# A cycle's first score bank read by ScalarE and VectorE in turn, in a fused attention and mixer kernel

## The chip, the cores and the metric

The kernel runs on one core of one Trainium2 chip. The metric is device microseconds of one execution; lower is better. Engines are named as in the profile: PE is TensorE's matmuls and PEld its weight loads, ACT is ScalarE, DVE is VectorE, POOL is GpSimd, SP is SyncE, which issues most DMAs.

## The reference, cut to what matters

The output is a gated sum of an attention branch (16 heads of 28 over 2048 tokens, one shared key and value head) and a token and channel mixer. The change lies in the attention alone:

```python
q = (x @ wq).reshape(B, S, H, Dh)...      # B, S, D, H = 1, 2048, 448, 16; Dh = 28
k = x @ wk
v = x @ wv
scores = jnp.einsum("bhqd,bkd->bhqk", q, k) * (Dh ** -0.5)
p = _softmax(scores, axis=-1)
o = jnp.einsum("bhqk,bkd->bhqd", p, v)
a = (o in token order).reshape(B, S, H * Dh) @ wo
return g * a + (1 - g) * b                # g = sigmoid(x . gate_w), b the mixer branch
```

## The kernel before

The first 390 us compute the projections and the mixer; they are the same in both kernels. The rest is attention, in 16 units `u` (four blocks of 512 queries by four groups of four heads). A unit has 16 key tiles of 128 keys. A cycle `c` handles two of them, so a unit is eight cycles `i` = 0 to 7, and there are 128 cycles (`NC`).

All engines run in the order in which the code is written; no scheduler reorders it. The score products of one key tile give four banks of 128 keys by 512 queries, one for each head, from three fp32r products each (L207: `qh,kh`, `ql,kh`, `qh,kl`). Eight banks of PSUM are in play: four single banks `s0` to `s3` (the profile names all of them `bank`) and two pairs (`pair`). Singles swap roles from cycle to cycle: this cycle's `s2, s3` are the next one's `s0, s1`.

A cycle does this:

1. PE: scores of the even tile into `s0`, `s1` and the first pair (twelve products); then scores of the odd tile into `s2`, `s3` and the second pair.
2. ACT: the exponentials of `s0`, `s1` (L260, into the tile `pa`), of `s2`, `s3` and the second pair (into `pb`), and last of `pa[:, both]` in place in SBUF, 1024 columns.
3. DVE copies the first pair raw into `pa[:, both]` (L1033), which is what ACT's last step then works on.
4. PE: the products with the values of the two key tiles of the cycle before (L969), for the left 256 queries into `s0[:, 0:256]`, then for the right 256 into `s1[:, 0:256]`. These overwrite scores that the exponentials have read. Then a "job" into `s0[:, 256:480]`: an eighth of a unit's product with `wo` (L919), or, in cycles 2 to 11, a quarter row of a mixer product left over (112 columns wide).
5. DVE adds the two value results to the running sum `o` (L892, or L888 for the first of a unit), then the job's result (L936, or L955).

At `i` = 2 (`MAX_AT`) of each unit PE also computes bounds of the next unit's maxima into the first pair, and DVE reduces them.

VectorE also has side work, each piece at one cycle of a unit, between the copy of step 3 and the first addition of step 5: the end of the maxima at `i` = 3 (L249, L250 and a transpose, then eight DMAs on SP's queue); the reciprocal of the softmax sums at `i` = 1 (L902) with two instructions of a range check (L877, L878); the product `norm` with the reciprocals at `i` = 4 (L914); at `i` = 5 the high part of the queries of the unit after next (L196), at `i` = 6 their low part (L199, 512 columns), and right after that the four DMAs that fetch the following queries `qr` on SP's queue (L192). The reciprocal's input `rt` is a DMA on the same queue (L897), issued at the end of `i` = 0; its result goes out (`rd`, L906) and comes back spread over partitions (`rb`, L908).

Of the kernel before, what the change touches and what calls it, by code (L numbers as in the profile page):

```python
# [9 lines left out]
F32 = mybir.dt.float32  # L10
# [7 lines left out]
P = 128  # L18
# [19 lines left out]
def f32(ap):  # L38
    return ap.bitcast(F32)
# [3 lines left out]
def gated_mix_kernel(  # L43
# [13 lines left out]
    nc = tc.nc  # L57
# [137 lines left out]
        qh_of[u], ql_of[u] = qh, ql  # L195
        nc.vector.tensor_copy(qh, qr_of[u])  # L196

    def q_low(u):
        nc.vector.tensor_sub(ql_of[u], qr_of.pop(u), f32(qh_of[u]))  # L199

    def scores(u, kt, ps):
        kh = kh_of[0]
# [40 lines left out]
                nc.vector.reduce_max(mr[:, j, t:t + 1], mk, axis=AX.X)  # L243
        mx_of[u] = mr

    def max_end(u):
        mr = mx_of.pop(u).rearrange("p j t -> p (j t)")
        mc = late.tile([P, 32], F32R, tag="mc", bufs=2, name=f"mc_{u}")
        nc.vector.tensor_scalar(mc[:, 0:16], mr, -1.0, None, op0=ALU.mult)  # L249
        nc.vector.scalar_tensor_tensor(mc[:, 16:32], mr, -1.0, f32(mc)[:, 0:16],  # L250
                                       op0=ALU.mult, op1=ALU.subtract)
        mrow = late.tile([P, 32], F32, tag="mrow", bufs=2, name=f"mrow_{u}")
        nc.vector.transpose(mrow, f32(mc))
        for k in range(2):
            rows = f32(qh_of[u])[DH + k:P:32, :].rearrange("j (t p q) -> p j t q", p=4, q=32)
            for p in range(4):
                nc.sync.dma_start(rows[p], mrow[32 * p + 16 * k:32 * p + 16 * k + 16, :])
# [587 lines left out]
    with tc.tile_pool(name="s3", bufs=1, reuse_waits="tile") as s3, \  # L845
# [14 lines left out]
        def q_fetch(u):  # L860
            if u < NU:
                q_load(u, qr)
# [12 lines left out]
        def check(inverse, c):  # L875
            g = good[:, c:c + inverse.shape[1]]
            nc.vector.scalar_tensor_tensor(g, inverse, LIMIT, g, op0=ALU.is_le, op1=ALU.min)  # L877
            nc.vector.scalar_tensor_tensor(g, inverse, 1 / LIMIT, g, op0=ALU.is_ge, op1=ALU.min)  # L878
# [18 lines left out]
            nc.sync.dma_start(rt, o[0:128:32, :].rearrange("j (a b) -> j a b", b=16))  # L897
            return u, o, rt

        def recip(u, o, rt, checked=True):  # L900
            rr = s3.tile([P, 16], F32, tag="rr", bufs=2, name=f"rr_{u}")
            nc.vector.reciprocal(rr, rt)  # L902
            if checked:
                check(rr.rearrange("p (a b) -> p a b", b=4), 0)
            rd = dram.tile([4, 512], F32, tag="rd", bufs=2, name=f"rd_{u}")
            nc.sync.dma_start(rd.rearrange("j (a b) -> (j a) b", b=16), rr)  # L906
            rb = s3.tile([P, 512], F32, tag="rb", bufs=2, name=f"rb_{u}")
            nc.sync.dma_start(rb, rd.unsqueeze(1).broadcast_to([4, 32, 512]))  # L908
            return u, o, rb

        def norm(u, o, rb):
            on_of[u] = s3.tile([P, 512], F32, tag="on", bufs=2, name=f"on_{u}")
            for cols in (slice(0, 256), slice(256, 512)) if u == NU - 2 else (slice(0, 512),):
                nc.vector.tensor_mul(on_of[u][:, cols], o[:, cols], rb[:, cols])  # L914

        def by_columns(ps, a, t, w, start=True, stop=True):
            for i in range(4):
# [58 lines left out]
        jobs += [(w4_products, w4_add, (n // 4,), quarters[n % 4]) for n in range(2 * sum(JOBS_0), 16)]  # L976
        assert len(jobs) == sum(JOBS_0) + 10
        left, right, both, front = slice(0, 1), slice(1, 2), slice(2, 4), slice(0, 2)
        sums, norms, later = [], [], []
        pv = None  # L980
        MAX_AT = 2

# [13 lines left out]
        def run_jobs(ps, n):  # L996
            job_adds(job_products(ps, n))

        NC = NU * NT // 2
        HINTS = {8 * NT // 2 + 4: [mybir.EngineType.SP],  # L1000
                 14 * NT // 2 - 2: [mybir.EngineType.DVE, mybir.EngineType.Activation]}
        for c in range(NC):
            u, i = divmod(c, NT // 2)
            k = 2 * c
            s0, s1, s2, s3_ = singles if c % 2 == 0 else singles[2:] + singles[:2]
            if c == 0:
                pb = score_tiles(u, 1, s2, s3_, s0, s1)
                for j, ps in enumerate((s2, s3_, s0, s1)):
                    exps(pb, slice(j, j + 1), ps.unsqueeze(1))
                pa = score_tiles(u, 2, *(q[:, h] for q in pairs for h in range(2)))  # L1010
                nc.vector.tensor_copy(pa[:, front], pairs[0])
                for ps, n in zip((s2, s3_), JOBS_0):
                    run_jobs(ps, n)
                exps(pa, both, pairs[1])
                exps(pa, front)
                pairs.reverse()
                continue
            if c > 1:
                pa = score_tiles(u, 2 * i, s0, s1, pairs[0][:, 0], pairs[0][:, 1])
                with tc.block() if c in HINTS else nullcontext():  # L1020
                    if c in HINTS:
                        tc.mark_branch_hint_location("redo", "LikelyTaken", HINTS[c])
                    exps(pa, left, s0.unsqueeze(1))
                exps(pa, right, s1.unsqueeze(1))
            if i == 2 and u == 0:
                q_begin(1)
            if i == 3 and u == 0:
                q_low(1)
                q_fetch(2)
            if u == NU - 1 and i == 3:  # L1030
                norm(*norms.pop())
            if 1 < c < NC - 1:
                nc.vector.tensor_copy(pa[:, both], pairs[0])  # L1033
            elif c > 1:
                exps(pa, both, pairs[0])
            if i == 3 and later:
                later.pop(0)()
            if i == 1 and sums:
                norms.append(recip(*sums.pop()))
            if i == 4 and norms:  # L1040
                norm(*norms.pop())
            if i == 5 and u + 2 < NU:
                q_begin(u + 2)
            if i == 5 and u == 0:
                nc.sync.dma_start(wof, wo.rearrange("(g p) n -> p g n", p=P))
            if i == 6 and u + 2 < NU:
                q_low(u + 2)
                q_fetch(u + 3)
            pb = score_tiles(u, 2 * i + 1, s2, s3_, pairs[1][:, 0], pairs[1][:, 1])
            exps(pb, left, s2.unsqueeze(1))  # L1050
            exps(pb, right, s3_.unsqueeze(1))
            exps(pb, both, pairs[1])
            if 1 < c < NC - 1:
                exps(pa, both)
            if u and i == (3 if u == NU - 1 else 4):
                jobs += [(wo_products, wo_add, (u - 1, t), cols) for t in range(4) for cols in halves]
            v = (c - 1) // (NT // 2)
            at_max = i == MAX_AT and u + 1 < NU
            q0, q1 = slice(0, 256), slice(256, 512)
            values((k - 2, k - 1), s0[:, q0], q0)  # L1060
            values_end(v, s0[:, q0], q0)
            if at_max:
                max_part(u + 1, range(4), pairs[0][:, 0])
                later.append(lambda u=u: max_end(u + 1))
            elif i == MAX_AT:
                run_jobs(pairs[0][:, 0], 1)
            values((k - 2, k - 1), s1[:, q0], q1)
            adds = job_products(s0[:, q1], 0 if c == 1 else 1)
            values_end(v, s1[:, q0], q1)
            if i == 0 and v < NU - 1:  # L1070
                sums.append(sums_begin(v))
            job_adds(adds)
# [75 lines left out]
        with tc.If(again > 0, label="redo"):  # L1148
            for b in range(NB):
                for g in range(NG):  # L1150
                    u = b * NG + g
                    q_fetch(u)
                    q_begin(u)
                    q_low(u)
                    max_full(u, bank)
                    max_end(u)
                    pv = banks.pop(0)
                    for kt in range(NT):
                        ps = [bank(f"s2_{u}_{kt}_{j}") for j in range(4)]
                        scores(u, kt, ps)  # L1160
                        p = s3.tile([P, 4, 512], F32, tag="p", bufs=PB, name=f"p2_{u}_{kt}")
                        for j in range(4):
                            exps(p, slice(j, j + 1), ps[j].unsqueeze(1))
                        for j in range(4):
                            nc.tensor.matmul(pv[32 * j:32 * j + 32, :], vext[:, kt, :], p[:, j],
                                             start=(kt == 0), stop=(kt == NT - 1), tile_position=(0, 32 * j))
                    values_end(u, pv)
                    banks.append(pv)
                    norm(*recip(*sums_begin(u), False))
# [59 lines left out]
```

## Time and profile before

| | before |
|---|---|
| median of 3 runs | 903.35 us (902.7 to 903.94) |
| the profiled execution's own time | 903.46 us |
| its span, first to last instruction | 901.7 us |
| PE busy in the span | 896.0 us (99%) |
| ACT busy | 629.8 us (70%) |
| DVE busy | 527.5 us (58%) |
| granted TensorE clock, mean | 0.999 |

The profile is of one execution. Its timeline rows give a start in microseconds, a duration, the engine, the line, the operation, the tiles and how many instructions are merged into the row; in square brackets stands how long the engine had been idle and what ended that. A busy PE need not be at its peak, since the ends of matmuls are modelled: a wait of TensorE is seen at the weight loads (PEld) and in the distance between the starts of its matmuls.

### The profile page before, as it was taken

What the parts mean: (1) busy time and instruction counts of PE and PEld (TensorE: products, weight loads), DVE (VectorE), ACT (ScalarE), POOL (GpSimd) and SP (SyncE); (2) the same over time, 40 slices, a digit from 0 to 9 for tenths busy, and PEclk for the clock granted to TensorE, in tenths of its full rate; (3) what the DMA queues carried; (4) which work ended last, traced back from release to release, by engine and by line L of the source; (5) the groups of instructions that cost most, each with busy time, mean ns of one, the idle gap of its engine ahead of it and who ended that gap; (6) DMA issues with size and microseconds to landing.
All of it is one profiled execution on the core that took longest, in us unless ns stands there. A gap on an engine that the chain in (4) does not pass through costs nothing.

```text
span 901.7 us, 24214 instructions
## 1 busy us (share of the span) xinstructions
PE 896.0 (99%) x10396; PEld 628.0 (70%) x10396; DVE 527.5 (58%) x983; ACT 629.8 (70%) x1002; POOL 70.5 (8%) x109
## 2 busy tenths in 40 slices
PE   9999999999999999999999999999999999999998
PEld 7898988888888888865555555555555555555554
DVE  5575555643342431156776776677667667777665
ACT  5453354322132231279999999999999999999995
POOL 1123300700000520020000000000000000000000
PEclk9999999999999999999999999999999999999999
DMA  9977755400300300001000001000011000010001
GB/s 309 332 173 207 201 180 129 108 1 1 88 2 1 88 0 1 1 22 55 25 15 25 13 25 46 24 25 16 25 34 41 20 15 25 15 56 14 15 15 44
DMA packets 50474, 54.77 MB, mean 61 GB/s; under 512 B 11804, under 2 KB 38028, under 8 KB 50252
## 3 DMA queue, kind: packets, MB, share of 16 engines
q1 hardware_dynamic: 47580, 47.74, 19.0%
q10 hardware_dynamic: 2784, 5.46, 1.6%
q8 instruction: 82, 1.34, 0.6%
q14 instruction: 28, 0.23, 0.1%
HBM read 36.35 MB, written 15.33 MB: 57 GB/s over the span
## 4 chain that ended last, share of the span: by engine, by line
PE 97%; ACT 1%; DMA 0%; DVE 0%; issue 0%
PE bank L969 26%; PE bank L207 19%; PE bank L919 5%; PE acc L769 5%; PE acc L767 5%; PE acc L768 5%; PE g L138 4%; PE g L139 4%; PE g L140 4%; PE pair L207 3%; PE hs L530 1%; PE hs L529 1%; PE g L141 1%; PE g L142 1%; ACT p L260 1%; PE hs L532 1%
## 5 line engine op out<-in xcount | busy, mean ns | idle before, releaser
L260 ACT ACTIVATE p<-bank 128x512 f32<-128x512 f32 x514 | 266.5, 608 | 4.5 <-POOL pick L942 1.5
L969 PE MATMUL bank<-p,vext 128*32 128x256 f32 x4064 | 247.6, 382 | 0.5
L969 PEld LDWEIGHTS bank<-p,vext 128*32 128x32 f32 x4064 | 117.6, 109 | 116.0 <-ACT p L260 52.8
L1033 DVE COPY p<-pair 128x1024 f32<-128x1024 f32 x125 | 153.0, 1224 | 57.2 <-PE pair L207 43.4
L757 ACT ACTIVATE gh<-g 128x512 fp32r<-128x512 f32 x55 | 32.9, 598 | 184.1 <-PE g L142 184.1
L892 DVE TENSOR_TENSOR o<-o,bank 128x256 f32<-128x256 f32 x222 | 93.5, 421 | 80.5 <-PE bank L969 70.3
L260 ACT ACTIVATE p<-p 128x1024 f32<-128x1024 f32 x126 | 138.3, 1097 | 0.0
L260 ACT ACTIVATE p<-pair 128x1024 f32<-128x1024 f32 x129 | 136.8, 1061 | 0.0
L759 DVE TENSOR_TENSOR gl<-gf,gh 128x512 fp32r<-128x512 f32 x55 | 40.5, 737 | 160.6 <-ACT gf L758 160.6
L207 PE MATMUL bank<-qh,kh 32*128 32x512 f32 x514 | 114.7, 444 | 0.0
L207 PE MATMUL pair<-qh,kh 32*128 32x512 f32 x510 | 114.0, 443 | 0.0
L207 PE MATMUL bank<-qh,kl 32*128 32x512 f32 x514 | 101.6, 389 | 0.0
L207 PE MATMUL bank<-ql,kh 32*128 32x512 f32 x514 | 101.3, 390 | 0.0
L207 PE MATMUL pair<-qh,kl 32*128 32x512 f32 x510 | 101.0, 389 | 0.0
L207 PE MATMUL pair<-ql,kh 32*128 32x512 f32 x510 | 100.5, 389 | 0.0
L207 PEld LDWEIGHTS bank<-qh,kh 32*128 32x128 f32 x514 | 47.4, 181 | 60.1 <-issue 38.1
L769 PE MATMUL acc<-w4h,gl 128*128 128x448 f32 x220 | 80.7, 367 | 0.0
L767 PE MATMUL acc<-w4h,gh 128*128 128x448 f32 x220 | 80.1, 364 | 0.0
L768 PE MATMUL acc<-w4l,gh 128*128 128x448 f32 x220 | 79.8, 363 | 0.0
L919 PE MATMUL bank<-wof,on 128*32 128x224 f32 (+1 forms) x976 | 68.9, 356 | 0.0
L138 PE MATMUL g<-ah,w3h 128*128 128x512 f32 x168 | 65.4, 389 | 0.0
L139 PE MATMUL g<-al,w3h 128*128 128x512 f32 x168 | 65.4, 389 | 0.0
(205 smaller groups left out, 1388.4 us busy)
## 6 DMA issues: line engine op xcount, KB each, us to landing
rb<-rd SPq DMA_DIRECT2D x15, 256.0 KB
x<-in_x_dram SPq DMA_DIRECT2D x4, 896.0 KB
hd<-raws SPq DMA_DIRECT2D x16, 224.0 KB
hraw<-hd SPq DMA_DIRECT2D x4, 896.0 KB
w34raw<-in_w_dram SPq DMA_DIRECT2D x7, 512.0 KB
qr<-qd SPq DMA_DIRECT2D x64, 56.0 KB
w34raw<-in_w_dram SPq DMA_DIRECT2D x7, 448.0 KB
out_dram<-ot SPq DMA_DIRECT2D x14, 224.0 KB
```

Source lines behind the costliest of these rows:

```text
L138: nc.tensor.matmul(ps, wh[:, c, :], ah[:, c, :], start=(c == 0), stop=False)
L139: nc.tensor.matmul(ps, wh[:, c, :], al[:, c, :], start=False, stop=False)
L207: nc.tensor.matmul(ps[j], k[h, keys], q[h, :], start=(r == 0), stop=(r == 2), tile_position=(32 * j, 0))
L260: nc.scalar.activation(p[:, heads], p[:, heads] if source is None else source, AF.Exp, scale=SCALE)
L759: nc.vector.tensor_sub(gl, gf, f32(gh))
L767: nc.tensor.matmul(ps, gh[:, tok], w4h[i][:, k, :], start=(f == 0), stop=False)
L768: nc.tensor.matmul(ps, gh[:, tok], w4l[i][:, k, :], start=False, stop=False)
L769: nc.tensor.matmul(ps, gl[:, tok], w4h[i][:, k, :], start=False, stop=(f == stop))
L892: nc.vector.tensor_add(o, o, pv)
L919: nc.tensor.matmul(ps[32 * i:32 * i + 32, :], a[:, c:c + 32], w, start=start, stop=stop, tile_position=(0, 32 * i))
L969: nc.tensor.matmul(pv[32 * j:32 * j + 32, :], vext[:, kt, :], p_of[k][:, j, qs], start=(k == ks[0]), stop=(k == ks[-1]), tile_position=(0, ...
L1033: nc.vector.tensor_copy(pa[:, both], pairs[0])
```

## The change

The first exponential of a cycle reads only columns 0 to 319 (`SHARE`) of `s0`. VectorE copies columns 320 to 511 of `s0` raw into `pa`, ahead of its copy of the pair, and ACT's last exponential of the cycle, in place in SBUF, covers those 192 columns too: 1216 instead of 1024. For that the 192 columns have to lie next to the pair's, so `s0` now holds the tile's second head and `s1` its first. The split is made in all cycles from 3 to 126 but those with `i` = 2 and cycle 123: 108 cycles.

VectorE's side work moves behind its first addition of values, and ahead of the second. The low part of the queries is made in two halves of 256 columns, the first at `i` = 6, the second at `i` = 0 of the next unit, and the four fetches of `qr` follow the second half. `norm` is done in halves at `i` = 3 and `i` = 7. The range check follows the first addition at `i` = 1; the reciprocal itself stays ahead of it. Of the end of the maxima the first instruction stays at `i` = 3, the other two and the eight DMAs go to `i` = 4. In the first unit the low part of the next queries is made at `i` = 3 and 5, and the load of `wof` comes at `i` = 6 instead of 5.

```diff
-    def q_low(u):
-        nc.vector.tensor_sub(ql_of[u], qr_of.pop(u), f32(qh_of[u]))
+    def q_low(u, cols=slice(0, 512)):
+        raw = qr_of.pop(u) if cols.stop == 512 else qr_of[u]
+        nc.vector.tensor_sub(ql_of[u][:, cols], raw[:, cols], f32(qh_of[u])[:, cols])
...
+        SHARE = 320
+        def side_work(u, i):
+            if i == 1 and checks:
+                check(checks.pop().rearrange("p (a b) -> p a b", b=4), 0)
+            if i == 3 and norms:
+                norm(*norms[0], q0)
+            if i == 7 and norms:
+                norm(*norms.pop(), q1)
+            if i == 4 and later:
+                max_end(*later.pop())
+            if u == 0 and i in (3, 5):
+                q_low(1, q0 if i == 3 else q1)
+                if i == 5:
+                    q_fetch(2)
+            if i == (6 if u == 0 else 5) and u + 2 < NU:
+                q_begin(u + 2)
+            if i == (7 if u == 0 else 6) and u + 2 < NU:
+                q_low(u + 2, q0)
+            if u and i == 0 and u + 1 < NU:
+                q_low(u + 1, q1)
+                q_fetch(u + 2)
...
             if c > 1:
-                pa = score_tiles(u, 2 * i, s0, s1, pairs[0][:, 0], pairs[0][:, 1])
+                pa = score_tiles(u, 2 * i, s1, s0, pairs[0][:, 0], pairs[0][:, 1])
+                split = 1 < c < NC - 1 and i != MAX_AT and not (u == NU - 1 and i == 3)
+                n0 = SHARE if split else 512
...
-                    exps(pa, left, s0.unsqueeze(1))
-                exps(pa, right, s1.unsqueeze(1))
+                    nc.scalar.activation(pa[:, 1, 0:n0], s0[:, 0:n0], AF.Exp, scale=SCALE)
+                exps(pa, left, s1.unsqueeze(1))
+                if split:
+                    nc.vector.tensor_copy(pa[:, 1, n0:512], s0[:, n0:512])
...
             if 1 < c < NC - 1:
                 nc.vector.tensor_copy(pa[:, both], pairs[0])
...
             if i == 3 and later:
-                later.pop(0)()
+                later.append((later[0], *max_begin(later.pop())))
             if i == 1 and sums:
                 norms.append(recip(*sums.pop()))
-            if i == 4 and norms:
-                norm(*norms.pop())
-            if i == 5 and u + 2 < NU:
-                q_begin(u + 2)
...
-            if i == 6 and u + 2 < NU:
-                q_low(u + 2)
-                q_fetch(u + 3)
...
             if 1 < c < NC - 1:
-                exps(pa, both)
+                rest = pa.rearrange("p j n -> p (j n)")[:, 512 + n0:2048]
+                nc.scalar.activation(rest, rest, AF.Exp, scale=SCALE)
...
             values((k - 2, k - 1), s0[:, q0], q0)
             values_end(v, s0[:, q0], q0)
...
+            side_work(u, i)
             values((k - 2, k - 1), s1[:, q0], q1)
```

The order of the instructions at three places, with the engines that each waits for. In the names, `p_5_10` is the tile `pa` of unit 5's cycle 5, `bank_0` to `bank_3` are the four singles (in cycle 5 `s0` is `bank_2`; in cycle 6, when the values of `p_5_10` are multiplied, it is `bank_0`), `pair_1` is the first pair; a wait on `Activation` is on ScalarE, one on `PE` on TensorE, one on `DMAHW` on a transfer.

VectorE in cycle 5 of unit 5, before:

```order
L1033 COPY p_5_10_6061<-pair_1_3228 128x1024 [waits PE_49]
L196 CAST qh_7_6065<-qr_3229 128x512 [waits DMAHW5_49,DMAHW6_49,DMAHW4_49,DMAHW3_49]
L892 TENSOR_TENSOR o_5_5829<-o_5_5829,bank_2_3181 128x256 [waits DVE_49,PE_49,Activation_49]
L892 TENSOR_TENSOR o_5_5829<-o_5_5829,bank_3_3182 128x256 [waits DVE_49,PE_49,Activation_49]
L936 SCALAR_TENSOR_TENSOR ot_4_6047<-bank_2_3181,gg_77,x1_70 128x224 [waits PE_49]
```

And in the changed kernel:

```order
L1057 COPY p_5_10_6108<-bank_2_3181 128x192 [waits Activation_49]
L1061 COPY p_5_10_6108<-pair_1_3228 128x1024 [waits PE_49]
L898 TENSOR_TENSOR o_5_5872<-o_5_5872,bank_2_3181 128x256 [waits PE_49]
L196 CAST qh_7_6139<-qr_3229 128x512 [waits DMAHW6_49,DMAHW7_49,DMAHW5_49,DMAHW4_49]
L898 TENSOR_TENSOR o_5_5872<-o_5_5872,bank_3_3182 128x256 [waits DVE_49,PE_49,Activation_49]
L942 SCALAR_TENSOR_TENSOR ot_4_6094<-bank_2_3181,gg_77,x1_70 128x224 [waits PE_49]
```

A copy of 192 columns stands ahead of the pair's copy and waits for ScalarE; the cast of the queries has gone from ahead of the first addition to behind it.

TensorE from the end of the odd tile's scores to the job, one cycle later, before:

```order
L207 MATMUL pair_0_3227<-qh_5_5060,kl_75 128x512 x2
L969 MATMUL bank_0_3179<-p_5_10_6061,vext_76 32x256 [waits Activation_49]
L969 MATMUL bank_0_3179<-p_5_10_6061,vext_76 32x256 x3
L969 MATMUL bank_0_3179<-p_5_11_6080,vext_76 32x256 x4
L969 MATMUL bank_1_3180<-p_5_10_6061,vext_76 32x256 [waits Activation_49]
```

And in the changed kernel:

```order
L208 MATMUL pair_0_3227<-qh_5_5116,kl_75 128x512 x2
L975 MATMUL bank_0_3179<-p_5_10_6108,vext_76 32x256 [waits DVE_49]
L975 MATMUL bank_0_3179<-p_5_10_6108,vext_76 32x256 x3
L975 MATMUL bank_0_3179<-p_5_11_6125,vext_76 32x256 x4
L975 MATMUL bank_1_3180<-p_5_10_6108,vext_76 32x256 [waits Activation_49]
```

The order is the same; the first value product of a cycle waits for VectorE where it waited for ScalarE.

SP's queue around the end of unit 8 (`rt_8` is the load of the softmax sums, `qr` the fetch of queries, `out` a store of finished rows), before:

```order
L192 DMA qr_3229<-qd_80 28x512 [waits DMAHW3_49,DVE_49]
L192 DMA qr_3229<-qd_80 28x512 [waits DMAHW4_49]
L192 DMA qr_3229<-qd_80 28x512 [waits DMAHW5_49]
L192 DMA qr_3229<-qd_80 28x512 [waits DMAHW6_49]
L939 DMA out_0_dram<-ot_5_6168 128x448 [waits DMAHW7_49,DVE_49]
L897 DMA rt_8_7787<-o_8_7335 128x1x16 [waits DMAHW0_49,DVE_49]
```

And in the changed kernel:

```order
L945 DMA out_0_dram<-ot_5_6213 128x448 [waits DMAHW3_49,DVE_49]
L192 DMA qr_3229<-qd_80 28x512 [waits DMAHW4_49,DVE_49]
L192 DMA qr_3229<-qd_80 28x512 [waits DMAHW5_49]
L192 DMA qr_3229<-qd_80 28x512 [waits DMAHW6_49]
L192 DMA qr_3229<-qd_80 28x512 [waits DMAHW7_49]
L903 DMA rt_8_7867<-o_8_7405 128x1x16 [waits DMAHW0_49,DVE_49]
```

The four fetches, two cycles ahead of the load of `rt` before, now stand right in front of it and are released in the same cycle.

More of the change, by code (lines that the diff above doesn't have):

```diff
@@ L244, in max_full, with max_begin @@
         mx_of[u] = mr
-    def max_end(u):
+    def max_begin(u):
         mr = mx_of.pop(u).rearrange("p j t -> p (j t)")
@@ L249, in max_end @@
         nc.vector.tensor_scalar(mc[:, 0:16], mr, -1.0, None, op0=ALU.mult)
+        return mr, mc
+    def max_end(u, mr=None, mc=None):
+        if mr is None:
+            mr, mc = max_begin(u)
         nc.vector.scalar_tensor_tensor(mc[:, 16:32], mr, -1.0, f32(mc)[:, 0:16],
@@ L898, in sums_begin, with recip @@
             return u, o, rt
-        def recip(u, o, rt, checked=True):
+        def recip(u, o, rt):
             rr = s3.tile([P, 16], F32, tag="rr", bufs=2, name=f"rr_{u}")
             nc.vector.reciprocal(rr, rt)
-            if checked:
-                check(rr.rearrange("p (a b) -> p a b", b=4), 0)
+            checks.append(rr)
             rd = dram.tile([4, 512], F32, tag="rd", bufs=2, name=f"rd_{u}")
@@ L909, in recip, with norm @@
             return u, o, rb
[L911 to L914, printed above, removed]
+        def norm(u, o, rb, *cols):
+            if not cols or cols[0].start == 0:
+                on_of[u] = s3.tile([P, 512], F32, tag="on", bufs=2, name=f"on_{u}")
+            for part in cols or (slice(0, 256), slice(256, 512)):
+                nc.vector.tensor_mul(on_of[u][:, part], o[:, part], rb[:, part])
         def by_columns(ps, a, t, w, start=True, stop=True):
@@ L978, in gated_mix_kernel @@
         left, right, both, front = slice(0, 1), slice(1, 2), slice(2, 4), slice(0, 2)
-        sums, norms, later = [], [], []
+        sums, norms, later, checks = [], [], [], []
         pv = None
@@ L999, in gated_mix_kernel @@
         NC = NU * NT // 2
+        SHARE = 320
+        q0, q1 = slice(0, 256), slice(256, 512)
         HINTS = {8 * NT // 2 + 4: [mybir.EngineType.SP],
                  14 * NT // 2 - 2: [mybir.EngineType.DVE, mybir.EngineType.Activation]}
+        def side_work(u, i):
[18 more added lines that the diff above has]
+                q_fetch(u + 2)
         for c in range(NC):
@@ L1022, in gated_mix_kernel @@
                         tc.mark_branch_hint_location("redo", "LikelyTaken", HINTS[c])
-                    exps(pa, left, s0.unsqueeze(1))
-                exps(pa, right, s1.unsqueeze(1))
[L1025 to L1029, printed above, removed]
+                    nc.scalar.activation(pa[:, 1, 0:n0], s0[:, 0:n0], AF.Exp, scale=SCALE)
+                exps(pa, left, s1.unsqueeze(1))
+                if split:
+                    nc.vector.tensor_copy(pa[:, 1, n0:512], s0[:, n0:512])
             if u == NU - 1 and i == 3:
@@ L1035, in gated_mix_kernel @@
                 exps(pa, both, pairs[0])
+            if i == 2 and u == 0:
+                q_begin(1)
             if i == 3 and later:
-                later.pop(0)()
+                later.append((later[0], *max_begin(later.pop())))
             if i == 1 and sums:
                 norms.append(recip(*sums.pop()))
-            if i == 4 and norms:
-                norm(*norms.pop())
-            if i == 5 and u + 2 < NU:
-                q_begin(u + 2)
-            if i == 5 and u == 0:
+            if i == 6 and u == 0:
                 nc.sync.dma_start(wof, wo.rearrange("(g p) n -> p g n", p=P))
-            if i == 6 and u + 2 < NU:
-                q_low(u + 2)
-                q_fetch(u + 3)
             pb = score_tiles(u, 2 * i + 1, s2, s3_, pairs[1][:, 0], pairs[1][:, 1])
@@ L1058, in gated_mix_kernel @@
             at_max = i == MAX_AT and u + 1 < NU
-            q0, q1 = slice(0, 256), slice(256, 512)
             values((k - 2, k - 1), s0[:, q0], q0)
@@ L1063, in gated_mix_kernel @@
                 max_part(u + 1, range(4), pairs[0][:, 0])
-                later.append(lambda u=u: max_end(u + 1))
+                later.append(u + 1)
             elif i == MAX_AT:
                 run_jobs(pairs[0][:, 0], 1)
+            side_work(u, i)
             values((k - 2, k - 1), s1[:, q0], q1)
@@ L1168, in gated_mix_kernel @@
                     banks.append(pv)
-                    norm(*recip(*sums_begin(u), False))
+                    norm(*recip(*sums_begin(u)))
                     for t in range(4):
```

## The prediction

> **What bounds the kernel now.** I read the page's busy shares first, then the windows of the attention stage, its waits, and one cycle in the timeline. The page, and a window of 100 us from the middle (its columns are length, then busy time of PE, PEld, DVE, ACT and POOL, clock, DMA share):
>
> ```profile
> PE 896.0 (99%) x10396; PEld 628.0 (70%) x10396; DVE 527.5 (58%) x983; ACT 629.8 (70%) x1002; POOL 70.5 (8%) x109
> ...
> 520.00:620.00 100.00, 100.00 (x1708) 56.46 (x1704) 70.92 (x137) 99.73 (x155) 0.00 (x0) 1.00 0.10 30
> ```
>
> In the attention stage both TensorE and ScalarE read as full, at a clock of 1.00, and VectorE is free for 29% of the time. Two full engines that feed each other can hide a short wait, so the waits come next, from 440 to 880 us:
>
> ```profile
> PEld bank L969 <- ACT p L260: 46.9, 113, 0.4
> ```
>
> Once a cycle the first value product waits for an exponential. The timeline shows which one, and how much of those 0.4 us is a loss. From the scores of one cycle to those of the next:
>
> ```profile
> 604.77 0.40 PE L207 MATMUL pair<-qh,kl 32*128 32x512 f32 x2
> ...
> 605.19 0.60 ACT L260 ACTIVATE p<-bank 128x512 f32<-128x512 f32 x1
> ...
> 605.27 1.23 DVE L1033 COPY p<-pair 128x1024 f32<-128x1024 f32 x1 [0.48 <-PE pair L207]
> ...
> 605.47 0.40 PE L207 MATMUL pair<-qh,kl 32*128 32x512 f32 x2
> ...
> 605.84 1.45 PEld L969 LDWEIGHTS bank<-p,vext 128*32 128x32 f32 x32 [0.41 <-ACT p L260]
> ...
> 607.03 0.42 DVE L892 TENSOR_TENSOR o<-o,bank 128x256 f32<-128x256 f32 x1 [0.54 <-PE bank L969]
> ...
> 607.51 0.21 PEld L919 LDWEIGHTS bank<-wof,on 128*32 128x32 f32 x8 [0.22 <-DVE o L892]
> ...
> 607.59 0.56 PE L919 MATMUL bank<-wof,on 128*32 128x224 f32 x8
> ...
> 607.90 0.42 DVE L892 TENSOR_TENSOR o<-o,bank 128x256 f32<-128x256 f32 x1 [0.44 <-PE bank L969]
> ...
> 608.08 0.18 PEld L207 LDWEIGHTS bank<-qh,kh 32*128 32x128 f32 x2 [0.36 <-issue]
> ...
> 608.24 0.44 DVE L936 SCALAR_TENSOR_TENSOR ot<-bank,gg,ot 128x224 f32<-128x224 f32 x1
> ...
> 609.08 2.07 ACT L260 ACTIVATE p<-bank 128x512 f32<-128x512 f32 x4
> ...
> 609.73 1.45 PEld L969 LDWEIGHTS bank<-p,vext 128*32 128x32 f32 x32 [0.42 <-ACT p L260]
> ```
>
> Call T the end of the even tile's scores, 604.77 + 0.40 = 605.17. The exponential of `s0` starts at 605.19 and ends at 605.79; 0.05 later, at V = 605.84, the values start. The period is 609.73 − 605.84 = 3.89 us, and V − T = 0.67. From V to the next T TensorE runs through values, job and scores without another wait that I can find (the job's weights wait for VectorE until 607.51, but its matmul starts 0.08 later, in step with those before it). So the period is (V − T) + 3.22.
>
> How early could V come? In a cycle near the start, where ScalarE was not in the way, the last score product and the first value product stand so:
>
> ```profile
> 399.35 0.40 PE L207 MATMUL pair<-qh,kl 32*128 32x512 f32 x2
> ...
> 399.68 0.85 PE L969 MATMUL bank<-p,vext 128*32 128x256 f32 x12
> ```
>
> That is 0.33 us from start to start even without a wait; in the cycle above it is 605.84 − 605.47 = 0.37. The wait for ScalarE thus costs 0.04 us a cycle, and V − T cannot go below 0.63. Over 100 cycles there are 4 us to win at that place.
>
> **The change part by part.** First the split. ScalarE's work stays what it was: six instructions a cycle over 4096 columns. What alters is the way from T to V. The order of the changed kernel, shown above, has the 192-column copy wait for ScalarE, and no instruction of ScalarE reads that bank but the first exponential; the first value product waits for that copy. Exponential and copy of the bank follow each other, then. Prices by groups of instructions, and by rows of an early stage in which VectorE waits for ScalarE:
>
> ```profile
> L260 ACT ACTIVATE p<-bank 128x512 f32<-128x512 f32 x514 | 266.5, 608 | 4.5 <-POOL pick L942 1.5
> ...
> L260 ACT ACTIVATE p<-pair 128x1024 f32<-128x1024 f32 x129 | 136.8, 1061 | 0.0
> ...
> L1033 DVE COPY p<-pair 128x1024 f32<-128x1024 f32 x125 | 153.0, 1224 | 57.2 <-PE pair L207 43.4
> ...
> L888 DVE COPY o<-bank 128x256 f32<-128x256 f32 x32 | 13.6, 424 | 7.5 <-PE bank L969 7.5
> ...
> 120.34 0.59 ACT L758 ACTIVATE gf<-g 128x512 f32<-128x512 f32 x1
> ...
> 120.97 0.69 DVE L759 TENSOR_TENSOR gl<-gf,gh 128x512 fp32r<-128x512 f32 x1 [1.98 <-ACT gf L758]
> ```
>
> - Exponential of 320 columns: (1061 − 608) / 512 = 0.885 ns a column, so 0.60 − 0.17 = 0.43 us.
> - ScalarE's end to VectorE's start: 120.97 − 120.93 = 0.04.
> - Copy of 192 columns: (1224 − 424) / 768 = 1.04 ns a column, 0.424 − 0.067 = 0.36.
> - VectorE's end to TensorE's load: 607.51 − 607.45 = 0.06.
>
> That is 0.89 us where 0.60 + 0.05 = 0.65 stood: V − T becomes 0.91, and a period 4.13. The change cuts 0.17 off the exponential and puts 0.46 behind it. **+0.24 us** in each of 100 cycles (of the 108, those from 12 on): +24.0 us. In the other eight (3 to 9, and 11) the job is a quarter row, TensorE has room and ScalarE takes some of the wait anyway; between 0 and 0.24 each I take half: +1.1.
>
> The bounds: an exponential in proportion to its columns, without a fixed part, is 0.37, and the nearest shorter PSUM instruction of VectorE is this one:
>
> ```profile
> L955 DVE SCALAR_TENSOR_TENSOR x<-bank,gi,x 128x112 f32<-128x112 f32 x10 | 3.3, 328 | 0.0
> ```
>
> With 0.37 and 0.33 the step is +0.14, or +14 us. With 0.42 for the copy (the 256-column row) and 0.49 for the exponential (what a whole one takes from start to start: 2.07 for four, less 0.60, over three) it is +0.36, or +36. I take 0.24, from slopes between two rows of the same instruction each.
>
> [...]
>
> Second, VectorE. A cycle of the kernel before with side work on it:
>
> ```profile
> 601.29 2.07 ACT L260 ACTIVATE p<-bank 128x512 f32<-128x512 f32 x4
> ...
> 601.37 1.22 DVE L1033 COPY p<-pair 128x1024 f32<-128x1024 f32 x1 [0.48 <-PE bank L207]
> ...
> 602.51 0.68 DVE L199 TENSOR_TENSOR ql<-qr,qh 128x512 fp32r<-128x512 f32 x1
> ...
> 603.14 0.42 DVE L892 TENSOR_TENSOR o<-o,bank 128x256 f32<-128x256 f32 x1
> ```
>
> The first addition starts 1.85 behind the exponential here and 607.03 − 605.19 = 1.84 in the cycle above, which has no side work: it costs nothing before, and there is nothing to win. In the changed kernel the pair copy starts at T + 0.49 + 0.27 (192 columns at 1.04 ns, and 0.07 between starts: additions of 256 columns stand 608.24 − 607.90 = 0.34 apart), and frees the engine 1.14 later (602.51 − 601.37), at T + 1.90. The first addition is due 1.19 after V (607.03 − 605.84), at T + 2.10. So 0.2 us are left, and the side work would no longer fit there; behind the first addition 0.53 are free (607.90 − 607.03 − 0.34). Into this go halves of 0.34, the two small instructions of the maxima, or one cast of 512 columns:
>
> ```profile
> L250 DVE SCALAR_TENSOR_TENSOR mc<-mr,mc 128x16 fp32r<-128x16 f32 x15 | 2.6, 176 | 0.5
> ...
> L253 DVE STREAM_TRANSPOSE mrow<-mc 128x32 f32<-128x32 f32 x15 | 3.2, 211 | 0.5
> ...
> L196 DVE CAST qh<-qr 128x512 fp32r<-128x512 f32 x15 | 6.7, 447 | 0.0
> ```
>
> All end inside the gap, so the moves cost nothing. Were the cover gone, the job's addition would be late and hold the next odd scores, 0.1 us a piece. The eight DMAs of the maxima go a cycle later on SP's queue, four cycles ahead of their use: nothing.
>
> Third, SP's queue at `i` = 0. Rows of the kernel before, the fetches in two units and the way of the sums:
>
> ```profile
> 603.22 1.61 SPq L192 DMA_DIRECT2D qr<-qd  x4
> ...
> 612.23 0.58 SPq L897 DMA_DIRECT2D rt<-o  x1
> ...
> 614.18 0.24 DVE L902 RECIPROCAL rr<-rt 128x16 f32<-128x16 f32 x1
> ...
> 614.45 0.34 SPq L906 DMA_DIRECT2D rd<-rr  x1
> ...
> 615.87 0.56 SPq L908 DMA_DIRECT2D rb<-rd  x1
> ...
> 634.47 2.53 SPq L192 DMA_DIRECT2D qr<-qd  x4
> ```
>
> In 13 units (1 to 13) the load of `rt` now stands behind the four fetches. The second half of the low part ends at T + 2.10 + 0.34 + 0.42 = 2.86, the fetches leave at 2.89 and take 1.61, and `rt` goes out at T + 4.54. It lands at most 1.95 later (614.18 − 612.23), and hardly under 1.42 (what the small `rd` took until `rb` could leave): T + 5.96 to 6.49. VectorE wants it at the next cycle's T + 1.90, that is T + 6.03. It stands there up to 0.46 us, with the first addition queued behind it and the job's weights behind that. The reciprocal's 0.24 fills the 0.2 us of room, and the job has 0.08 to spare: a loss of 0 to 0.42 in a unit, 0.2 as the middle, +2.6 us. In three units the fetches took longer (2.53 is the longest); I add 1.8 for such.
>
> The sum: 24.0 + 1.1 + 2.6 + 1.8 = 29.5 us on the profiled execution's 903.46, or **933.0 us**; the median of the runs lies 0.1 lower, which I leave out.
>
> **The rivals.**
>
> *Both engines read the bank at once, and V comes early.* If the copy's wait ended before the exponential's end (because its part does not hang on ScalarE's), V would be held by the scores alone, V − T = 0.63, and 100 cycles would win 0.04: 903.46 − 4 = 899. For it: in the rows above exponential and pair copy start within 0.08 us of each other. Against it: they read different banks, and the added instruction names ScalarE as what it waits for. Its point of decision is whether the first value product starts 0.63 or 0.91 after T. [...] I give it 0.06.
>
> *The shorter exponential pays for the copy.* With a copy of 0.12 us including its release, V − T would stay at 0.67: 903. No instruction of VectorE from PSUM in these rows is under 0.3 us. 0.03.
>
> *The sums' load decides beside the split.* If `rt` always lands at its late bound and slow fetches are the rule behind the moved half (0.92 more, 2.53 − 1.61), each of 13 units loses up to 1.3 us: 24 + 1.1 + 13 × 0.42 + 13 × 0.5 for half of them slow = 37, or 940. For it: it is a queue that the change itself fills. Against: most fetches took 1.61. 0.09.
>
> **How the numbers follow.** The forecast gets 0.82. Its own bounds are 903.5 + 14 + 0.5 = 918 and 903.5 + 36 + 1.1 + 5 = 945.6; the late `rt` lies within, and what is left out is the two rivals on the other side and the ends. Range 918 to 945. A measurement of this kernel can tell about 0.2% (1.8 us) from no change. Faster 0.06, same 0.03, slower 0.91.
>
> **What would show it.** The first value product's weights should wait for VectorE's 192-column copy, not for ScalarE, and the period in the middle should be 4.1 us; ScalarE should idle 0.2 to 0.4 us a cycle ahead of its first exponential, since its six instructions fit into 3.89 now. The copy should take 0.36 and start 0.04 behind the exponential's end. At `i` = 1 the reciprocal should wait for a DMA. I am wrong if copy and exponential overlap, if the value products still wait for ScalarE, or if cycles with side work are longer than their neighbours by more than 0.1 us.

## The result, and the profile after

| | before | changed |
|---|---|---|
| median of 6 runs each | 903.2 us (902.7 to 903.94) | 936.31 us (935.61 to 936.71) |
| ratio, with its 95% interval | | 1.0365 [1.0351, 1.0378] |
| span of the profiled execution | 901.7 us | 934.7 us |
| granted TensorE clock, mean | 0.999 | 0.999 |

The change costs 33.1 us, 3.7%; the prediction said 933.0 us, 918 to 945. First the page of the changed kernel, its busy engines and its chain:

```profile
PE 901.5 (96%) x10396; PEld 631.2 (68%) x10396; DVE 555.6 (59%) x1120; ACT 634.1 (68%) x1002; POOL 71.2 (8%) x109
...
PE 83%; DVE 5%; ACT 5%; DMA 4%; issue 1%; SPq 1%; ACTq 0%; DVEq 0%
```

And the same 100 us window of the attention stage as before, in its columns:

```profile
520.00:620.00 100.00, 95.40 (x1596) 53.94 (x1592) 72.37 (x154) 94.73 (x145) 0.00 (x0) 1.00 0.08 27
```

TensorE and ScalarE, both full before, are idle for 5% now, at the same clock of 1.00: neither became slower (an exponential of 512 columns takes 0.604 us on average after 0.602, a value product 0.382 in both), both wait. The waits from 440 to 880 us say for what (columns: total us, times, longest):

```profile
DVE p L1057 <- ACT p L1054: 81.1, 93, 0.9
PEld bank L975 <- DVE p L1057: 60.8, 93, 0.7
...
ACT p L1054 <- PE pair L208: 20.2, 79, 1.2
...
DVE rr L908 <- DMA rt<-o: 4.7, 12, 1.0
```

Read as a ring: the value products wait for VectorE's 192-column copy (before: 46.9 us for ScalarE at that place), the copy waits for the first exponential, and that one waits, 0.26 us a time, for the scores that TensorE delivers late because its values began late. One cycle in the timeline:

```profile
611.61 0.40 PE L208 MATMUL pair<-qh,kl 32*128 32x512 f32 x2
...
612.04 0.44 ACT L1054 ACTIVATE p<-bank 128x320 f32<-128x320 f32 x1 [0.21 <-PE pair L208]
...
612.51 0.36 DVE L1057 COPY p<-bank 128x192 f32<-128x192 f32 x1 [0.86 <-ACT p L1054]
612.79 1.22 DVE L1061 COPY p<-pair 128x1024 f32<-128x1024 f32 x1
612.92 1.45 PEld L975 LDWEIGHTS bank<-p,vext 128*32 128x32 f32 x32 [0.66 <-DVE p L1057]
...
617.06 0.37 PEld L975 LDWEIGHTS bank<-p,vext 128*32 128x32 f32 x12 [0.66 <-DVE p L1057]
```

T is 611.61 + 0.40 = 612.01 and V is 612.92: V − T = 0.91. Exponential 0.44, 0.03 to the copy, copy 0.36, 0.05 to TensorE's load, one after the other. The next V is 4.14 later; over all plain cycles the period's median is 4.133 us, against 3.891 before.

The 33.0 us between the two spans, from the distances between the V of successive cycles: the 100 plain split cycles (those from 12 on) +24.2; the early ones +1.3; the cycle `i` = 1, with the reciprocal, +4.6 in 13 units; the first unit after its `i` = 5, +2.06; and +0.8 ahead of the attention stage, in code that is the same. The last three need rows. The unit with the largest loss at the reciprocal:

```profile
627.25 2.34 SPq L192 DMA_DIRECT2D qr<-qd  x4
...
629.46 1.45 PEld L975 LDWEIGHTS bank<-p,vext 128*32 128x32 f32 x32 [0.66 <-DVE p L1057]
...
629.69 0.58 SPq L903 DMA_DIRECT2D rt<-o  x1
...
631.58 0.25 DVE L908 RECIPROCAL rr<-rt 128x16 f32<-128x16 f32 x1 [1.04 <-DMA rt<-o]
...
632.16 0.16 PEld L925 LDWEIGHTS bank<-wof,on 128*32 128x32 f32 x8 [1.25 <-DVE o L894]
...
634.34 0.59 PEld L975 LDWEIGHTS bank<-p,vext 128*32 128x32 f32 x16 [0.42 <-ACT p L1054]
```

The load of `rt` leaves right behind the four fetches and lands 1.89 us later; the reciprocal stands 1.04 us for it, the first copy of values behind it, and the job's weights behind that. This unit's cycle takes 4.88 us, where the same cycle without the wait takes 3.90 (experiment three); its fetches took 2.34 us, and most others lost about 0.26 with fetches near 1.6.

In the first unit stands a wait that the prediction does not have:

```profile
410.60 4.82 SPq L263 DMA_DIRECT2D qh<-mrow  x8
...
416.51 0.42 DVE L200 TENSOR_TENSOR ql<-qr,qh 128x256 fp32r<-128x256 f32 x1 [2.36 <-DMA qh<-mrow]
...
417.18 0.33 DVE L961 SCALAR_TENSOR_TENSOR x<-bank,gi,x 128x112 f32<-128x112 f32 x1
...
417.56 0.50 PE L208 MATMUL bank<-qh,kh 32*128 32x512 f32 x2 [1.95 <-DVE x L961]
```

The maxima's eight DMAs write rows of `qh`, now at `i` = 4. In this unit alone the second half of the low part, which reads that `qh`, follows at `i` = 5. It waits 2.36 us, and TensorE stands 1.95 us ahead of the next scores. Before, the low part of the same queries was made whole ahead of these DMAs, so it had nothing to wait for:

```profile
402.44 0.68 DVE L199 TENSOR_TENSOR ql<-qr,qh 128x512 fp32r<-128x512 f32 x1
...
404.87 4.62 SPq L257 DMA_DIRECT2D qh<-mrow  x8
```

The 0.8 us ahead of the attention stage come before 130 us. At 99 us the changed kernel's instructions run 0.57 us ahead of the same ones before; from 130 us to the attention stage they stand 0.81 behind. In between ScalarE waits longer for the load of `xr`. The waits from 95 to 135 us, before and changed:

```profile
ACT ah L705 <- DMA xr<-xd: 4.1, 2, 3.0
ACT ah L711 <- DMA xr<-xd: 6.7, 1, 6.7
```

The change does not touch this load. Whether it is late in every execution, one trace of each kernel can't tell.

### The profile page after: what moved, and what is told of

Its sections match the earlier page's. It is cut to its first block, busy times and chain, and to the rows that moved or that the text cites. A ratio compares the mean times of both kernels' runs of the same rounds, so it can differ in the third digit from the quotient of the medians.

```text
span 934.7 us, 24305 instructions
## 1 busy us (share of the span) xinstructions
PE 901.5 (96%) x10396; PEld 631.2 (68%) x10396; DVE 555.6 (59%) x1120; ACT 634.1 (68%) x1002; POOL 71.2 (8%) x109
## 4 chain that ended last, share of the span: by engine, by line
PE 83%; DVE 5%; ACT 5%; DMA 4%; issue 1%; SPq 1%; ACTq 0%; DVEq 0%
PE bank L975 24%; PE bank L208 13%; PE bank L925 5%; PE acc L775 5%; PE acc L773 5%; PE acc L774 5%; ACT p L1054 5%; PE g L138 4%; PE g L140 4%; PE g L139 4%; DVE p L1057 4%; DMA rt<-o 2%; PE g L141 1%; PE g L142 1%; PE pair L208 1%
## 5 line engine op out<-in xcount | busy, mean ns | idle before, releaser
L266 ACT ACTIVATE p<-bank 128x512 f32<-128x512 f32 x388 | 203.8, 604 | 5.1 <-PE pair L208 2.0
L1061 DVE COPY p<-pair 128x1024 f32<-128x1024 f32 x125 | 152.0, 1216 | 7.6 <-PE pair L208 7.1
L1078 ACT ACTIVATE p<-p 128x1216 f32<-128x1216 f32 (+1 forms) x125 | 153.6, 1229 | 0.0
L1057 DVE COPY p<-bank 128x192 f32<-128x192 f32 x108 | 38.6, 358 | 93.0 <-ACT p L1054 93.0
L1054 ACT ACTIVATE p<-bank 128x320 f32<-128x320 f32 (+1 forms) x126 | 58.1, 461 | 27.4 <-PE pair L208 22.5
```

Source lines behind the costliest of these rows:

```text
L266: nc.scalar.activation(p[:, heads], p[:, heads] if source is None else source, AF.Exp, scale=SCALE)
L1054: nc.scalar.activation(pa[:, 1, 0:n0], s0[:, 0:n0], AF.Exp, scale=SCALE)
L1057: nc.vector.tensor_copy(pa[:, 1, n0:512], s0[:, n0:512])
L1078: nc.scalar.activation(rest, rest, AF.Exp, scale=SCALE)
```

## The experiments

The theory: the bank is read by two engines in turn, so the split puts a copy and one more hand-over, 0.40 us together, on the path and takes only 0.17 off it; the rest is the queue of SP and one wait in the first unit. Rivals: that moved side work, not the split, makes the loss; and that reading one bank by two engines slows a reader beyond the order of the two.

### One: the side work moved, no split

```diff
-                split = 1 < c < NC - 1 and i != MAX_AT and not (u == NU - 1 and i == 3)
+                split = False
```

> The changed kernel with the split taken out: the first exponential reads all 512 columns again, VectorE copies no part of that bank, and the side work stays in its new places. If the hand-over from ScalarE to VectorE in front of the value products is what costs (the series theory), 24 of the 33 us go, the period of a plain cycle is 3.89 us again, and what stays is the load of the softmax sums behind four fetches: it lands 1.89 us after its issue, later in terms of the shorter cycle than in the changed kernel, about 0.6 us lost in each of 13 units, and 2 us once in unit 0: 903.2 + 8 + 2 = 913, between 908 and 917. If the new order of the side work is the main cost (first rival), this kernel keeps at least 20 of the 33 us: 923 or more.

Measured: 917.73 us (915.74 to 918.49), ratio 1.0147 [1.0132, 1.0163], a little over the 908 to 917 that were expected. Waits from 440 to 880 us:

```profile
PEld bank L975 <- ACT p L1054: 46.9, 111, 0.5
...
DVE rr L908 <- DMA rt<-o: 13.7, 12, 1.9
```

The value products are back at before's 46.9 us, and the plain period at 3.900. The reciprocal's wait is three times that of the changed kernel: 8.9 us lost at `i` = 1, most units 0.54. Without the split VectorE's pair copy starts 0.08 us behind T instead of 0.78, so the engine comes to the reciprocal sooner by more than the load does, which moves with V alone (0.24). The first unit loses 4.2, where 2 were expected: 3.1 in the wait for the DMAs, in which TensorE stands still for 2.61 us, and 1.1 right after it, because the granted clock falls. The window behind that wait (its last three columns are clock, DMA share and GB/s), here and in the changed kernel:

```profile
417.80:421.30 3.50, 3.50 (x36) 1.51 (x36) 1.23 (x3) 2.35 (x4) 0.00 (x0) 0.51 0.62 159
417.80:421.30 3.50, 3.50 (x64) 1.95 (x60) 2.53 (x5) 2.69 (x4) 0.00 (x0) 1.00 0.58 153
```

At half the clock TensorE does 36 matmuls in the time of 64. So the moved side work, without the split, costs 14 us, and 13 of them begin at waits for DMAs, not at work on VectorE.

### Two: the side work mended, no split

The edit of experiment one, the fetches put behind the load of `rt`, and the first unit's steps out of each other's way:

```diff
-            if i == 4 and later:
+            if i == (5 if u == 0 else 4) and later:
                 max_end(*later.pop())
-            if u == 0 and i in (3, 5):
+            if u == 0 and i in (3, 4):
...
-                if i == 5:
+                if i == 4:
                     q_fetch(2)
...
                 q_low(u + 1, q1)
-                q_fetch(u + 2)
...
                 sums.append(sums_begin(v))
+                if u + 1 < NU:
+                    q_fetch(u + 2)
```

> The kernel without the split, and with two things of the side work put right: the four fetches are issued behind the load of the softmax sums instead of in front of it, and in unit 0 the low part of the queries is finished before the DMAs of the maxima are issued. The series theory has the halves of the side work fit into the gap between the additions, so nothing is left: 903.2, within 1.5 us of the kernel before. If the order of the side work on VectorE costs by itself (first rival), 910 or more.

Measured: 907.07 us (905.48 to 907.36), ratio 1.0032 [1.0020, 1.0044]. The reciprocal's wait and the first unit's are gone, 10.7 of the 14 us; but 3 us more than before remain, which was not expected. By the distances between V: 1.5 ahead of the attention stage, about 1 in four single stalls, and 9 ns in every plain cycle. The last is followed up in experiments eight and nine.

### Three: the split kept, the side work mended

The edits of experiment two without its first, so that the split stays.

> The changed kernel with the split, but the four fetches issued behind the load of the softmax sums, and unit 0's low part of the queries finished before the DMAs of the maxima. If the load of the sums costs 0.26 us in each of 13 units and one unit more, as the trace has it (4.4 us in all), and unit 0's wait 1.9 us, this is 936.3 - 6.3 = 930.0, from 929 to 931.5, with no wait of the reciprocal for a DMA. If SP's queue had no part in it, 936.

Measured: 930.54 us (929.37 to 931.21), ratio 1.0279 [1.0256, 1.0301], as expected. The same place of the timeline as in the changed kernel:

```profile
625.02 0.57 SPq L903 DMA_DIRECT2D rt<-o  x1
625.63 1.78 SPq L192 DMA_DIRECT2D qr<-qd  x4
...
627.63 0.24 DVE L908 RECIPROCAL rr<-rt 128x16 f32<-128x16 f32 x1
```

With the load ahead of the fetches the reciprocal waits for nothing, and the cycle `i` = 1 takes 3.90 us. The plain period is 4.133 still. Queue and first unit are thus some 6 of the 33 us. Of the 27.8 us by which this trace is still longer than the one before, 25.7 are the split (24.4 in the plain cycles, 1.3 in the early ones) and 1.9 lie ahead of the attention stage.

### Four: the split with the copy from another bank

This kernel leaves out the raw scores of the 192 columns and takes others in their place; it is for the time alone. To the edits of experiment three:

```diff
-                    nc.vector.tensor_copy(pa[:, 1, n0:512], s0[:, n0:512])
+                    nc.vector.tensor_copy(pa[:, 1, n0:512], pairs[0][:, 0, n0:512])
```

> The mended kernel with the split, but VectorE copies its 192 columns from the pair's first bank instead of the single bank (the output is wrong in these columns; the work is the same in size and kind on every engine). The copy then waits for TensorE alone, next to the exponential. The series theory has the whole price in the order of the two readers of one bank: here the value products start 0.63 us after the scores and the period is 3.85, so 899, from 897 to 902. If the copy, the wider last exponential or VectorE's load cost by themselves (second rival), it stays 10 us or more above the kernel before: 913 or more.

Measured: 899.58 us (899.36 to 901.4), ratio 0.9960 [0.9947, 0.9974], as expected. Two cycles of its timeline:

```profile
603.04 0.44 ACT L1053 ACTIVATE p<-bank 128x320 f32<-128x320 f32 x1
...
603.08 0.36 DVE L1056 COPY p<-pair 128x192 f32<-128x192 f32 x1 [0.46 <-PE pair L208]
...
603.62 1.45 PEld L975 LDWEIGHTS bank<-p,vext 128*32 128x32 f32 x32 [0.36 <-ACT p L1053]
...
607.48 1.23 PEld L975 LDWEIGHTS bank<-p,vext 128*32 128x32 f32 x27 [0.37 <-ACT p L1053]
```

And its window:

```profile
520.00:620.00 100.00, 99.94 (x1720) 57.04 (x1716) 77.62 (x165) 99.52 (x156) 0.00 (x0) 1.00 0.10 31
```

The same instructions with the same sizes, on the same engines; only the source of the copy differs. It starts 0.04 behind the exponential's start instead of 0.03 behind its end. V − T is 0.63 and the period 3.85. One edit takes 31 us away from experiment three (930.54 to 899.58; 29 by the ratios to the kernel before, 1.0279 to 0.9960, each taken on its own chip). Of that, 28.6 us are in the 100 plain cycles. The loss is neither the added instruction nor VectorE's load: it is that the copy comes after the exponential, for which the program makes it wait where both read one bank.

### Five and six: another share

`SHARE` is 448 in one and 256 in the other, all else as in the changed kernel.

```diff
-        SHARE = 320
+        SHARE = 448
```

> The changed kernel with 448 columns for ScalarE and 64 for VectorE. Series theory: the exponential grows by 128 x 0.83 ns = 0.106 us, the copy shrinks by 128 x 1.04 = 0.133, so the period shrinks by 0.027 and 108 cycles win 2.9 us: 933.4, from 932 to 935. Most of the price is then the second instruction's fixed part and release, which a smaller part doesn't remove. If the price went with the columns that VectorE takes (a contention of the two readers, second rival), two thirds of the 24 us would go: 920.

> The changed kernel with 256 columns for each. Series theory: the exponential shrinks by 64 x 0.83 = 0.053, the copy grows by 64 x 1.04 = 0.067: the period grows by 0.013, 1.4 us in all, 937.7, from 936.5 to 939.5. If exponential and copy ran side by side, so that the longer of them counts, even parts would be better than 320 and 192: 930 or less.

Measured: 936.44 us (933.96 to 937.39), ratio 1.0340 [1.0313, 1.0367], for 448, and 938.88 us (938.23 to 940.36), 1.0379 [1.0355, 1.0403], for 256; the second is as expected, the first above its range. Groups from 440 to 880 us (busy, then mean ns; idle before, and for whom) of the changed kernel, with 320:

```profile
L1054 ACT ACTIVATE p<-bank 128x320 f32<-128x320 f32 x93 | 40.8, 438 | 17.7 <-PE pair L208 14.3 <-PE bank L208 2.2
L1057 DVE COPY p<-bank 128x192 f32<-128x192 f32 x93 | 33.3, 358 | 81.1 <-ACT p L1054 81.1
```

With 448:

```profile
L1054 ACT ACTIVATE p<-bank 128x448 f32<-128x448 f32 x94 | 51.2, 545 | 16.1 <-PE pair L208 13.0 <-PE bank L208 1.7
...
L1057 DVE COPY p<-bank 128x64 f32<-128x64 f32 x94 | 21.1, 225 | 91.9 <-ACT p L1054 91.9
```

With 256:

```profile
L1057 DVE COPY p<-bank 128x256 f32<-128x256 f32 x92 | 39.1, 425 | 75.3 <-ACT p L1054 75.3
...
L1054 ACT ACTIVATE p<-bank 128x256 f32<-128x256 f32 x92 | 35.3, 384 | 18.7 <-PE pair L208 14.3 <-PE bank L208 3.2
```

The two durations add to 796 ns at 320, 770 at 448 and 809 at 256: −26 and +13. The periods moved by −27 and +13 ns (4.106 and 4.146 us). Two reads in turn, then, and nothing else: a contention of the readers that the small copy would have eased by the 0.16 us a cycle that a total of 920 asks for isn't there. Moving columns between the engines hardly matters (0.84 against 1.04 ns a column, from these rows); the fixed part of the second instruction does: 225 ns for 64 columns, of which only 67 go with the columns. The total at 448 was 3 us above what was expected while its plain cycles cost 21.8 us, as foretold: 2.8 us were lost ahead of attention (0.8 in the changed kernel) and 5.8 at the reciprocal (4.6). At 256 the plain cycles cost 25.7, 1.4 more, as foretold; its first unit loses 3.8 us with the clock at half as in experiment one, and 0.5 us are won ahead of attention.

### Seven: the split alone

The kernel before with the split, its side work where it was:

```diff
-                pa = score_tiles(u, 2 * i, s0, s1, pairs[0][:, 0], pairs[0][:, 1])
+                pa = score_tiles(u, 2 * i, s1, s0, pairs[0][:, 0], pairs[0][:, 1])
+                split = 1 < c < NC - 1 and i != MAX_AT and not (u == NU - 1 and i == 3)
+                n0 = 320 if split else 512
...
-                    exps(pa, left, s0.unsqueeze(1))
-                exps(pa, right, s1.unsqueeze(1))
+                    nc.scalar.activation(pa[:, 1, 0:n0], s0[:, 0:n0], AF.Exp, scale=SCALE)
+                exps(pa, left, s1.unsqueeze(1))
+                if split:
+                    nc.vector.tensor_copy(pa[:, 1, n0:512], s0[:, n0:512])
...
-                exps(pa, both)
+                rest = pa.rearrange("p j n -> p (j n)")[:, 512 + n0:2048]
+                nc.scalar.activation(rest, rest, AF.Exp, scale=SCALE)
```

> The kernel before with the split alone; the side work stays ahead of the first addition. The series theory has 25 us for the split, and then VectorE's room of 0.2 us ahead of the first addition too small for the side work: 0.35 us lost in each of four cycles of a unit, 0.07 in a fifth, 1.5 us in 14 or 15 units: 903.2 + 25 + 21 = 949, from 940 to 955. If the new order of the side work is what costs (first rival), this kernel is near 903 to 910.

Measured: 948.84 us (948.61 to 950.23), ratio 1.0501 [1.0485, 1.0517], as expected. The cycle `i` = 4, with `norm` in its old place:

```profile
612.43 1.22 DVE L1037 COPY p<-pair 128x1024 f32<-128x1024 f32 x1
...
612.57 1.45 PEld L969 LDWEIGHTS bank<-p,vext 128*32 128x32 f32 x32 [0.67 <-DVE p L1028]
...
613.56 0.68 DVE L914 TENSOR_TENSOR on<-o,rb 128x512 f32<-128x512 f32 x1
...
614.16 0.89 DVE L892 TENSOR_TENSOR o<-o,bank 128x256 f32<-128x256 f32 x2
...
614.63 0.16 PEld L919 LDWEIGHTS bank<-wof,on 128*32 128x32 f32 x8 [0.61 <-DVE o L892]
```

The first addition, due 1.19 after V at 613.76, starts at 614.16, and the job's weights go 2.06 after V, not 1.67. The cycle takes 4.47 us; `i` = 7, without side work, takes 4.133. All plain cycles together lose 37.8 us, against 24.2 with the side work moved. So in the plain cycles the move is worth 13.6 us where the split is; where it is not, it wins nothing (experiments two and nine).

### Eight and nine: the heads exchanged, and the side work with the old heads

Experiment two had 9 ns a cycle left over with no split. One thing was still different in it: which head's scores lie in `s0`. Eight is the kernel before with that alone; the last line exchanges the order of the two exponentials to match:

```diff
-                pa = score_tiles(u, 2 * i, s0, s1, pairs[0][:, 0], pairs[0][:, 1])
+                pa = score_tiles(u, 2 * i, s1, s0, pairs[0][:, 0], pairs[0][:, 1])
...
-                    exps(pa, left, s0.unsqueeze(1))
-                exps(pa, right, s1.unsqueeze(1))
+                    exps(pa, right, s0.unsqueeze(1))
+                exps(pa, left, s1.unsqueeze(1))
```

Nine is experiment two with these lines as in the kernel before:

```diff
-                pa = score_tiles(u, 2 * i, s1, s0, pairs[0][:, 0], pairs[0][:, 1])
+                pa = score_tiles(u, 2 * i, s0, s1, pairs[0][:, 0], pairs[0][:, 1])
...
+                exps(pa, left, s0.unsqueeze(1))
+                exps(pa, right, s1.unsqueeze(1))
```

> The kernel before with only the two single heads of the even tile exchanged: the bank that ScalarE reads first now takes the tile's second head, whose products TensorE issues second. The series theory with the trace of the mended side work says that the first exponential starts 8 ns later after the scores, the period is 3.900 instead of 3.891, and 125 cycles cost 1.1 us: 0.1% over the kernel before. If the exchange costs nothing and the mended side work's 3 us are the side work's, the ratio is 1.000 and the period 3.891.

> The mended side work without the split and with the heads in their old order. If the halves of the side work fit into the gap between the additions, the period is 3.891 us and the time that of the kernel before, within 0.2%. If the moved side work costs by itself, it stays 0.3% over the kernel before, with a period over 3.895.

Measured: 905.27 us (904.26 to 906.66), ratio 1.0016 [1.0006, 1.0026], and 905.04 us (903.9 to 906.73), 1.0012 [1.0003, 1.0021], both as expected. The same two V, 72 cycles apart, in the kernel before:

```profile
515.94 1.45 PEld L969 LDWEIGHTS bank<-p,vext 128*32 128x32 f32 x32 [0.41 <-ACT p L260]
...
797.26 0.81 PEld L969 LDWEIGHTS bank<-p,vext 128*32 128x32 f32 x20 [0.42 <-ACT p L260]
```

And with the heads exchanged:

```profile
516.84 1.45 PEld L969 LDWEIGHTS bank<-p,vext 128*32 128x32 f32 x32 [0.43 <-ACT p L260]
...
798.84 1.24 PEld L969 LDWEIGHTS bank<-p,vext 128*32 128x32 f32 x28 [0.42 <-ACT p L260]
```

282.00 against 281.32 us: 9 ns a cycle. The first exponential starts 35 ns behind the end of the even scores (median), where it was 26; the products of its bank are now issued second. In nine the period is back at 3.891; what it has over before is 1.85 us ahead of attention and 1 us in four single stalls of 0.26 to 0.31 us, at cycles where experiment two has them too. What causes these wasn't found.

## Why the prediction was right, and where it was not

**The split, +0.24 us × 100: right in mechanism and size.** V − T was to go from 0.67 to 0.91 and went from 0.677 to 0.917 (medians); each of the four pieces came within 0.01: exponential 0.438 for 0.43, hand-over 0.03 for 0.04, copy 0.358 for 0.36, release 0.05 for 0.06. The sum is 24.2 us for 24.0. The four pieces alone make 0.23 us more than before (0.88 for 0.65); the other 0.01, 0.9 us in all, is the exchange of the heads, which the prediction did not price. That its rounding came out 0.01 high covered this by luck. (Its 0.46 us "behind" the exponential holds 0.06 of release, in place of 0.05 before; what is new on the path was to be 0.40 and is 0.39.)

**The early cycles, +1.1:** they lost 1.3.

**Side work in halves, nothing: right for VectorE.** In experiment three the cycles with side work (`i` = 0, 3, 4, 5 and 6) have the same median as `i` = 7, which carries half of `norm` alone, 4.13 us, and the no-split kernels stand at 3.89 to 3.90 in all of them; experiment seven shows what stood behind that term: left in its old place, the same work costs 13.6 us.

**The load of `rt`, +2.6 and +1.8: right in mechanism, the sum partly by luck.** It lands after 1.89 us, between the bounds of 1.42 and 1.95; all together 4.6 us are lost instead of 4.4. But the usual loss is about 0.27 instead of 0.2, 3.6 us in 13 units, and the slow fetches add 1.0 instead of 1.8: two units had them (1.85 and 2.34 us), and the worst lost 0.98. The two misses offset each other. Experiment three, which changes the queue's order, takes the loss away.

**"The eight DMAs of the maxima go a cycle later on SP's queue, four cycles ahead of their use: nothing": this step failed.** It holds in every unit but the first, where the low part is made at `i` = 3 and 5 and its second half waits 2.36 us behind those DMAs. About 1.9 us, once. The diff shows the first unit's own places; the prediction read the general ones. By the prediction's own sign, a cycle with side work over 0.1 us longer than its neighbours, the mechanism is wrong at this one place.

**The rivals.** That both engines read the bank at once did not happen, but its price was right: with another bank, V − T is the foretold 0.63 and the time 899.58 for 899. The order of the instructions makes the copy wait for ScalarE, and no run here has ScalarE and VectorE in that bank at the same time, so what the chip would do then is not shown. That a shorter exponential pays for the copy falls with the 64-column copy, whose 0.225 us is more than that rival's 0.12 with its release. That the sums' load decides, at 12 us, falls with the 4.6 us that it cost.

The sum came out 3.5 us low: 2.1 for the first unit, 0.6 in the three terms above, 0.8 ahead of attention. No reading of the change could foretell the last: the trace puts it at the load of `xr`, and the same code took from 0.5 us less to 2.8 us more than before in the traces of this study.

## What to carry to other kernels

Before two engines share the reading of a bank, ask whether they read it in turn: then the second part pays a whole instruction and one more hand-over on the path (here 0.39 us for 192 columns that saved 0.16), and none of the three shares tried here mends it. With the copy from another bank the same instructions cost nothing and win the last 0.04 us a cycle (experiment four); a correct kernel whose split lies over two banks was not built here. And where DMAs are moved, follow each to its reader in the first and last rounds of the loop, not in the middle alone, and put the one that someone waits for ahead of those that nobody does.

## What the runs showed that was not expected

The order in which the score products of two banks are issued moves the first exponential by 9 ns a cycle, 1 us in all, though they run side by side (in experiment eight they start within 0.02 us of each other and take 0.39 to 0.50 each) and nothing else changes (experiments eight and nine). Code ahead of the attention stage, the same in all kernels, took from 0.5 us less to 2.8 us more than before; with one trace of each kernel, a difference between programs can't be told from one between executions. The granted clock fell to 0.50 for about 3.4 us in the first unit of experiments one and six, after TensorE had stood still for 2.61 and 1.93 us; after 1.95 us in the changed kernel and in the one with 448 columns it stayed at 1.00, so the length of the wait alone does not decide. And single stalls of 0.26 to 0.31 us appear in experiments two and nine at the same four cycles, where VectorE's additions come late; the traces don't say why.
